# A new step order for an attention and gated feed-forward kernel, with the last value loads split in two

## The chip, the cores and the metric

The kernel runs on one core of a Trainium2 chip. The metric is the device time of one execution in microseconds (us). Time before: a median of 424.13 us over three runs (424.1, 424.13 and 425.38).

## The reference

Eight sequences of 448 tokens, twelve heads of 64. Queries and keys are normalised by their root mean square, attention follows, and its output (3584 rows of 768) goes through a feed-forward layer with a gate h * clip(h + 3, 0, 6) / 6 between two matrix products.

```python
q_n, k_n = rmsnorm(q, g_q), rmsnorm(k, g_k)               # q, k, v: (8, 12, 448, 64)
scores = matmul(q_n, k_n.transpose(0, 1, 3, 2)) / sqrt(64)
attn = softmax(scores)
x = matmul(attn, v) -> rows (8*448, 12*64)
h = x @ w_in                                              # (3584, 768) @ (768, 2048)
out = (h * clip(h + 3, 0, 6) / 6) @ w_out                 # (3584, 2048) @ (2048, 768)
```

## The kernel before

The unit of attention is a pair of heads; there are 48 pairs P, six for each sequence b. The kernel first builds a list of 2386 numbered steps (`Plan.add`), each with its kind, the engines that it may run on, and the steps that it depends on. Then `Plan.emit` puts them out in the order that the table `ORDER` gives; the table `WAY` says for a step which of its allowed engines it takes (0, the first one, if it isn't named). Every engine works off its own steps strictly in that order, so a step that waits holds up all that stands behind it on its engine. `ORDER` was written by a search outside the kernel; step numbers in this document are the numbers in these tables.

The kinds of steps that matter here:

- `ld`: SyncE (SP) issues one load of two heads' q, k or v, 256 KB (line 420). The order of loads on SP's queue is part of `ORDER`. q and k land in rings of six buffers `qk`, v in six buffers `vf`; for pairs 5 and 6 they land in space that later belongs to `gT` and `xT`.
- `sq`, `sqh` (squares, lines 362 on ACT and 364 on POOL), `red1`, `red2`, `redh` (sums, DVE, lines 449 and 483), `ln` and `ex` (the root by logarithm and exponential, ACT, lines 425 and 428), `sc`, `sch` (scaling, line 367, POOL or DVE): the normalisation of a pair.
- `tr`, `trh` (TensorE transposes, line 537) with `ck`, `cq` (copies out), and from pair 13 on `dt` (a DMA transpose issued by SP, line 556) with `kt` (a scaling of the keys in place on DVE or ACT, lines 566 and 564): the transposed q and k.
- `s` and `e`: scores of a block of keys on TensorE (lines 612 and 589) and their exponential on ACT (lines 617 and 595). The scores are two matmuls of 64 rows each, side by side in the array; every other matmul uses all rows.
- `cv`: the values to bf16 in `va` (line 346 on DVE, 348 on ACT, 352 on POOL), and `av`, `avh`: exponentials times values on TensorE (lines 675 and 634), then `rd`, `xn` (the division, DVE), and a transpose into `xT` (`xt`, `xth` on TensorE, `dx` by DMA, line 701).
- `h1`, `h3` (lines 748 and 767) with `relu` (ACT, line 726) and `gate` (DVE, line 729), `y384` (line 789) with `cy384` (copies on ACT or DVE, lines 348 and 350) and the store `st` (line 810): the feed-forward layer. Its matmuls fill TensorE's time between the attention steps of the next sequence.

The first sequence is done in two half passes over the queries (`prep_first`, `score_first`, `av_first`), so that TensorE gets work early; the weights are loaded by POOL meanwhile. Thirty `warm` matmuls on zeros run while nothing else is ready. Score banks (two, and a third one `X` shared with `av`) and two banks `M` for `h` and `y` are handed on by data dependencies: a score waits until `e` has read its bank, an `h3` until `gate` has.

Of the kernel before, what the change touches and what calls it, by code (L numbers as in the profile page):

```python
# [204 lines left out]
def kernel(  # L205
# [11 lines left out]
    nc = tc.nc  # L217
# [4 lines left out]
    NP = B * NPAIR  # L222
# [107 lines left out]
    for t in T_r:  # L330
        nc.vector.memset(t[:, S2:], 0.0)
    for t in eT_r:
        nc.vector.memset(t[:, :, S2:], 0.0)

    NPT = 13
    NXB = 2
    YA = 3
    NSP = 2
    NW0 = 8
    NW1 = 22  # L340

    plan = Plan()
# [65 lines left out]
    def load(P, parts=(0, 1, 2)):  # L408
        b, j = divmod(P, NPAIR)
        hs = slice(2 * j, 2 * j + 2)  # L410
        for i in parts:
            src = (q, k, v)[i]
# [544 lines left out]
```

## Time and profile before

| what | value |
|---|---|
| median of three runs | 424.13 us |
| the profiled execution | 425.55 us, of which the profile's span is 423.8 us |
| TensorE (PE) busy | 414.8 us, 98%, 3960 matmuls |
| ACT, DVE, POOL busy | 287.1, 225.8 and 178.1 us |
| granted TensorE clock over the span | 1.00 |
| data moved | 67.77 MB, 160 GB/s on average |
| fetches of instructions on queue q8 | 31 packets, 0.51 MB |

How to read it: an engine's share is an average over stages. TensorE is busy almost everywhere except at the very start, in a few stretches of the first 90 us and after the last matmul; ACT is busiest from 10 to 40 us and again around 100 us. The profile's marks such as `[1.55 <-DMA qk<-in_q_dram]` behind an instruction give the engine's idle time before it and what ended that. Busy times of matmuls overlap (they are pipelined), so a matmul's cost is taken below from the distance between the starts of neighbouring ones.

### The profile page before, as it was taken

Reading aid. Unit: us, or ns where it says so; the run is one execution under the profiler, and the core shown is the slowest. Engines: PE = TensorE matmul, PEld = TensorE weight load, DVE = VectorE, ACT = ScalarE, POOL = GpSimd, SP = SyncE. Lnnn points to the kernel's source line nnn. Section 1 sums busy time; section 2 is a strip of 40 time slices with the busy share of each in tenths; the row PEclk is TensorE's granted clock in tenths of the full one; section 3 lists DMA queues with packets and bytes.
Section 4 is the critical chain, followed back from the end, with each engine's and each line's share of the span. In section 5 each row is a group of like instructions: output and inputs, shape, how many; then the busy total and the mean of one; then the engine's idle time right before and its main releaser. Section 6 shows DMA issues by size and latency. Waiting matters only on the chain.

```text
span 423.8 us, 9991 instructions
## 1 busy us (share of the span) xinstructions
PE 414.8 (98%) x3960; PEld 243.0 (57%) x3960; DVE 225.8 (53%) x453; ACT 287.1 (68%) x523; POOL 178.1 (42%) x206
## 2 busy tenths in 40 slices
PE   7999999989999999999999999999999999999996
PEld 3566877645555555555555555555555555555564
DVE  5988774769775476565445455543453433232310
ACT  6999988789987768787767867666846662133101
POOL 3999685678774462593035655333030200000000
PEclk9999999999999999999999999999999999999999
DMA  7999999999869958595768469273144202200323
GB/s 249 292 282 220 244 216 170 274 267 274 207 155 267 249 129 226 172 197 144 198 154 239 110 159 215 79 184 77 40 106 112 57 26 60 43 7 0 109 68 118
DMA packets 98931, 67.77 MB, mean 160 GB/s; under 512 B 53156, under 2 KB 95428, under 8 KB 98884
## 3 DMA queue, kind: packets, MB, share of 16 engines
q1 hardware_dynamic: 93248, 60.50, 54.6%
q0 software_dynamic: 5248, 6.29, 9.0%
q8 instruction: 31, 0.51, 0.5%
q10 hardware_dynamic: 388, 0.34, 0.3%
q14 instruction: 16, 0.13, 0.1%
HBM read 50.23 MB, written 11.01 MB: 145 GB/s over the span
## 4 chain that ended last, share of the span: by engine, by line
PE 84%; DMA 6%; ACT 4%; issue 1%; DVE 1%; SPq 1%; POOL 1%; DVEq 0%; POOLq 0%; ACTq 0%
PE M L767 28%; PE M L789 27%; PE X L675 9%; PE S L589 5%; PE S L789 5%; PE X L589 3%; PE M L748 3%; DMA qk<-in_q_dram 3%; ACT eT L617 3%; DMA w_in_sb<-in_moe_w_in_dram 2%; DMA vf<-in_v_dram 1%; PE X L767 1%; PE S L767 1%; POOL qks L367 1%; PE X L789 1%
## 5 line engine op out<-in xcount | busy, mean ns | idle before, releaser
L367 POOL TENSOR_TENSOR qks<-qk,rs 112x512 bf16<-112x512 f32 (+1 forms) x88 | 88.9, 1024 | 119.5 <-ACT rs L428 94.8
L789 PE MATMUL M<-w_out_sb,gT 128*128 128x384 bf16 x752 | 138.0, 326 | 0.0
L767 PE MATMUL M<-xT,w_in_sb 128*128 128x448 bf16 x618 | 134.0, 353 | 0.0
L789 PEld LDWEIGHTS <-gT 128*128 128x128 bf16 x912 | 84.2, 98 | 58.3 <-issue 7.3
L729 DVE SCALAR_TENSOR_TENSOR gT<-ts,M 128x448 bf16<-128x448 f32 x119 | 73.3, 616 | 74.5 <-ACT ts L726 74.3
L595 ACT ACTIVATE eT<-S 112x896 bf16<-112x896 f32 x112 | 99.7, 916 | 6.9 <-PE X L675 3.6
L726 ACT ACTIVATE ts<-M 128x448 f32<-128x448 f32 x119 | 64.9, 546 | 46.5 <-PE M L767 39.4
L767 PEld LDWEIGHTS <-w_in_sb 128*128 128x128 bf16 x672 | 60.3, 98 | 58.2 <-issue 11.9
L364 POOL TENSOR_TENSOR sq<-qk 112x512 f32<-112x512 f32 (+1 forms) x59 | 59.1, 1012 | 24.1 <-DMA qk<-in_q_dram 9.6
L595 ACT ACTIVATE eT<-X 112x896 bf16<-112x896 f32 x56 | 51.3, 917 | 20.2 <-PE X L589 19.2
L675 PEld LDWEIGHTS <-eT 112*128 112x128 bf16 x1344 | 52.3, 97 | 15.1 <-DVE va L346 1.5
L675 PE MATMUL X<-va,eT 112*128 112x65 bf16 x1344 | 55.3, 193 | 1.4 <-DVE va L346 1.1
L449 DVE TENSOR_REDUCE ssq<-sq 112x16 f32<-112x1024 f32 x42 | 50.7, 1212 | 7.1 <-ACT sq L362 3.8
L589 PE MATMUL S<-T 64*128 64x448 bf16 x224 | 34.1, 353 | 0.1
L350 DVE COPY y<-M 128x384 f32<-128x384 f32 x23 | 12.8, 557 | 39.1 <-PE M L789 39.1
L694 DVE TENSOR_TENSOR xn<-X,rd 112x512 bf16<-112x512 f32 x42 | 28.9, 689 | 2.1 <-DMA xT<-xn 1.3
L691 DVE RECIPROCAL rd<-X 112x8 f32<-112x8 f32 x42 | 8.7, 207 | 38.2 <-PE X L675 35.4
L589 PEld LDWEIGHTS <-T 64*128 64x128 bf16 x336 | 12.3, 94 | 24.0 <-issue 18.8
L362 ACT ACTIVATE sq<-qk 112x512 f32<-112x512 f32 (+1 forms) x38 | 22.2, 595 | 5.6 <-DMA qk<-in_q_dram 3.4
L348 ACT COPY y<-M 128x384 f32<-128x384 f32 x24 | 11.5, 480 | 19.0 <-PE M L789 18.7
L748 PE MATMUL M<-xT,w_in_sb 128*128 128x224 bf16 x192 | 23.1, 259 | 0.2 <-DMA w_in_sb<-in_moe_w_in_dram 0.2
L789 PE MATMUL S<-w_out_sb,gT 128*128 128x384 bf16 (+1 forms) x128 | 22.3, 316 | 0.0
(88 smaller groups left out, 303.1 us busy)
## 6 DMA issues: line engine op xcount, KB each, us to landing
qk<-in_k_dram SPq DMA_DIRECT2D x45, 256.0 KB, 4.2
qk<-in_q_dram SPq DMA_DIRECT2D x45, 256.0 KB, 4.0
vf<-in_v_dram SPq DMA_DIRECT2D x45, 256.0 KB, 4.3
w_in_sb<-in_moe_w_in_dram POOLq DMA_DIRECT2D x4, 768.0 KB, 8.5
w_out_sb<-in_moe_w_out_dram POOLq DMA_DIRECT2D x4, 768.0 KB, 9.2
out_dram<-y SPq DMA_DIRECT2D x7, 336.0 KB, 3.9
out_dram<-y SPq DMA_DIRECT2D x8, 288.0 KB, 3.5
out_dram<-y SPq DMA_DIRECT2D x8, 240.0 KB, 2.7
```

The source lines that it names most:

```text
L364: em(nc.gpsimd.tensor_tensor(out=out, in0=in_, in1=in_, op=A_MULT))
L367: em((nc.vector if e == DVE else nc.gpsimd).tensor_tensor(out=out, in0=in_, in1=by.unsqueeze(3).to_broadcast(list(in_.shape)), op=A_MULT))
L449: em(nc.vector.tensor_reduce(out=ssq[:].rearrange("p i n -> p (i n)"), in_=sq[:].rearrange("p i (n d) -> p (i n) d", d=D), axis=AX_X, op=A ...
L589: em(nc.tensor.matmul(out=ps[:, a, 0:S], lhsT=qkT[r, S + t * TP:S + t * TP + 128], rhs=qkT[r, 0:S], start=True, stop=True))
L595: em(nc.scalar.activation(out=eT[:, t, 0:S2].rearrange("p (a s) -> p a s", a=2), in_=ps[0:TP, :, 0:S], func=EXP, bias=0.0, scale=1.0))
L675: em(nc.tensor.matmul(out=X_ps[:, a, i * E1:(i + 1) * E1], lhsT=eT[:, t, c:c + 128], rhs=va[:, a, t, :], start=(t == 0 and i == 0), stop=( ...
L694: em(nc.vector.tensor_tensor(out=xn[:].rearrange("p i a d -> p a i d"), in0=view()[:, :, :, 0:D], in1=rd[:].unsqueeze(3).to_broadcast([TP, ...
L726: em(nc.scalar.activation(out=ts[:], in_=ps()[:, 0:S], func=RELU, bias=0.5, scale=1.0 / 6.0))
L729: em(nc.vector.scalar_tensor_tensor(out=out, in0=shape(ts[:]), scalar=1.0, in1=shape(ps()[:, 0:S]), op0=A_MIN, op1=A_MULT))
L748: em(nc.tensor.matmul(out=ps()[:, f * SH:(f + 1) * SH], lhsT=w_in_sb[:, kt, f0:f0 + 128], rhs=xT[:, kt, z * SH:(z + 1) * SH], start=(kt == ...
L767: em(nc.tensor.matmul(out=ps()[:, 0:S], lhsT=w_in_sb[:, kt, f * 128:(f + 1) * 128], rhs=xT[:, kt, :], start=(kt == 0), stop=(kt == NKT - 1)))
L789: em(nc.tensor.matmul(out=ps()[:, 0:nc0], lhsT=gT[:, f, i * 128:(i + 1) * 128], rhs=w_out_sb[:, f, c0:c0 + nc0], start=(f == 0), stop=(f = ...
```

## The change

The list of steps and their dependencies stays as it was. Three things change.

1. `ORDER` and `WAY` are replaced by tables from another search, in a model that counts TensorE's instruction fetches and takes a third load that is issued right behind two others as late. Nearly all of the order differs in detail; the stages follow each other as before.
2. 123 steps run on another engine. The net of it: POOL gives away six `cv`, three `sq`, one `sqh` and two `sch` and takes two `sc`; ACT takes six `cv`, three `sq` and one `sqh` more; `kt` and `cy384` change engines in equal numbers.
3. The loads of v for the last three pairs (steps 1875, 1901 and 1927, pairs 45 to 47) become two DMAs each, one for each head.

```diff
     NPT = 13
     NXB = 2
+    NSL = 3
     YA = 3
...
-            def fn(_, dst=dst, src=src, np=np):
+            split = i == 2 and P >= NP - NSL
+
+            def fn(_, dst=dst, src=src, np=np, split=split):
                 rows = src[b, hs].rearrange("h (p t) d -> p h (t d)", t=T)
                 rows = bass.AP(rows.tensor, rows.offset, [[rows.ap[0][0], np]] + [list(d) for d in rows.ap[1:]])
-                em(nc.sync.dma_start(out=dst, in_=rows))
+                for h in ((0, 1) if split else (slice(0, 2),)):
+                    em(nc.sync.dma_start(out=dst[:, h], in_=rows[:, h]))
```

Some of what the tables change, by step. "Work ahead" is the TensorE work, in us, of all matmul steps that stand before the step in `ORDER`: the sum of their streaming times and 0.096 us for each change between scores and other matmuls.

| step | what it is | engine before, after | work ahead before | work ahead after |
|---|---|---|---|---|
| 10, 11 | loads of q and k of pair 1 | SP | 10 third, 11 fourth load | 11 third, 10 fourth load |
| 59, 60 | `ln`, `ex` for the first half of pair 0's queries | ACT | behind `sqh` 69 (reads load 10) | ahead of `sq` 68 (reads load 11) |
| 62 | `sch` of the same queries | POOL, DVE | 3.1 | 2.8 |
| 147 | load of v of pair 6 | SP | 20.5 | 20.1 |
| 346 | `cv` of pair 6 | DVE | 31.3 | 23.5 |
| 369 | load of v of pair 12 | SP | 71.6 | 65.3 |
| 589 | `cv` of pair 12 | DVE, POOL | 75.8 | 74.1 |
| 762 | first `av` of pair 12 | PE | 77.2 | 75.4 |
| 812 | `dt` of pair 16 | SP | 76.1 | 78.7 |
| 813 | `kt` of pair 16 | DVE | 81.9 | 82.8 |

Changes between scores and other matmuls in TensorE's order: 180 before, 170 after, 8 of the 10 fewer within the first 40 us of work.

279 rows, old and new, of tables (ORDER, WAY) are left out of this document.

## The prediction

> **What bounds the kernel now.** First the page: the span, TensorE's busy share, the slices.
>
> ```profile
> span 423.8 us, 9991 instructions
> ...
> PE 414.8 (98%) x3960; PEld 243.0 (57%) x3960; DVE 225.8 (53%) x453; ACT 287.1 (68%) x523; POOL 178.1 (42%) x206
> ...
> PE   7999999989999999999999999999999999999996
> ```
>
> TensorE is the bound, and a new order takes no matmul away. So I measured what an order can touch: from the starts of all 3960 matmuls I took each form's shortest distance to the next start (189 ns for an `h3` matmul, 161 for `y384`, 29 for `av`). Their sum is 384.8 us. The first matmul starts at 1.2, the last at 419.8; the 33.6 us between sum and reality are all there is. Part of that is the change between the scores' 64-row matmuls and the others, in the timeline of TensorE:
>
> ```profile
> 117.59 0.35 PE L589 MATMUL S<-T 64*128 64x448 bf16 x2
> 117.88 1.31 PE L767 MATMUL M<-xT,w_in_sb 128*128 128x448 bf16 x6
> 119.12 0.36 PE L589 MATMUL X<-T 64*128 64x448 bf16 x2
> ```
>
> Two scores side by side take 0.29 us to the next start instead of 0.19, six L767 1.24 instead of 6 x 0.189 = 1.13: some 96 ns a change. 180 changes x 0.096 = 17.3 us. The remaining 16.3 us lie, by start: 5.1 before 16 us, 1.9 to 28, 1.8 to 40, 1.2 to 60, 0.4 to 80, 1.6 to 100, and 4.2 thinly over the rest (no single wait above 0.12). The chain of waits, in order of time, names the two places with a cause:
>
> ```profile
> 1.77 5.09 DMA qk<-in_q_dram
> ...
> 82.44 6.31 DMA vf<-in_v_dram
> 89.61 1.15 PE X L675 x32
> ```
>
> The first, in the timeline of the start:
>
> ```profile
> 6.88 0.42 ACT L362 ACTIVATE sq<-qk 112x256 f32<-112x256 f32 x1 [1.55 <-DMA qk<-in_q_dram]
> 7.20 0.19 ACT L425 ACTIVATE rs<-ssq 112x4 f32<-112x4 f32 x1
> ...
> 8.38 0.47 PE L537 MATMUL M<-identity,qks 112*128 112x112 bf16 x6 [1.05 <-POOL qks L367]
> ```
>
> Load 10, the third, lands 5.1 us after issue; the first two took 2.7 and 2.9. `sqh` 69 waits for it 1.55 us at the head of ACT's queue, and `ln` 59, whose sum was there at 5.49, stands behind. The second is the largest single wait after 16 us:
>
> ```profile
> 88.86 0.69 DVE L346 TENSOR_SCALAR_CACHE_REDUCE va<-vf 112x512 bf16<-112x512 f32 x1 [2.35 <-DMA vf<-in_v_dram]
> ...
> 89.61 0.57 PE L675 MATMUL X<-va,eT 112*128 112x65 bf16 x13 [1.08 <-DVE va L346]
> ```
>
> Load 369 was issued at 82.44, too late for `cv` 589; TensorE lost 1.26 us by the starts. The stretches show what bounds the early stage:
>
> ```profile
> 10.00:20.00 10.00, 9.18 (x124) 5.11 (x126) 9.68 (x25) 9.94 (x26) 8.55 (x12) 1.00 1.07 307
> 20.00:30.00 10.00, 9.85 (x184) 6.71 (x182) 8.28 (x29) 9.90 (x17) 9.23 (x14) 1.00 0.98 263
> 30.00:40.00 10.00, 9.32 (x146) 6.71 (x142) 8.26 (x25) 9.71 (x17) 9.94 (x11) 1.00 1.10 246
> ```
>
> The columns after the length are PE, PEld, DVE, ACT, POOL, clock, DMA share, GB/s: ACT is full from 10 to 40 us, TensorE's "busy" there includes waits.
>
> **The change, part by part.** The sum is made against the profiled execution (425.55, of which 423.8 span); the median is 1.42 lower, and I carry the difference over to it.
>
> *Early stage, to about 44 us.* In the new order `ln` 59 and `ex` 60 stand ahead of the first reader of the third load, and `sch` 62 moves to an idle DVE. The first transposes come perhaps 1.3 us earlier. But ACT still restarts only with the third load, and it is the full engine. So I added up ACT's queue from that point, each step by its spacing back to back (`e` 0.80, `sq` 0.52, `sqh` 0.31, `ck` 0.52, `cv` 0.51, `relu` 0.42, `ln` and `ex` 0.11). Up to `e` step 536, at 43.71 before: 34.58 us of queue in 36.83 elapsed, so 2.25 of slack. New queue to the same step: 35.17. Bounds: all slack gone, 6.88 + 35.17 = 42.05, a gain of 1.66; all slack kept, a loss of 0.59. Slack was 0.9 by 23 us, where ACT is fullest; the rest came after. I take a third of it closed: -0.75 + 0.59, say **-0.2**. The 8 mode changes fewer here hide behind ACT.
>
> *The value load of pair 6.* `cv` 346 on DVE moves from 31.3 to 23.5 us of TensorE work, load 147 hardly. Between the load's issue and `cv` ACT has five `e` and three roots, 4.3 us, where 11.8 us lay between the two before. Loads around 28 us landed in 5.3 to 6.0 us. So DVE should wait 1.0 to 1.7 us at step 346, and behind it are `cq` 375, `rd` 335, `xn` 336, `ck` 377, which feed TensorE's next steps. DVE is 83% busy there and part is made up. Bounds 0 and 1.7; I take **+0.5**, as the loads that compete may also be fewer by then.
>
> *44 to 87 us.* 1.6 us less the switches' share remain, the largest 0.46 at 54.13 (an `av` waiting for `e`). The new order has POOL some 2.5 us of steps ahead at 60 us. Bounds 0 and -1.4; half of it, **-0.7**.
>
> *The wait at 88 us.* From load 369 to `cv` 589 there were 4.2 us of TensorE work (6.4 by the clock) against a landing of 6.31; now 8.8. The wait goes: **-1.2**. Next late: `dt` 812 to `kt` 813, 5.8 us of work before and 4.1 now, while that transpose landed in 5.1. DVE may wait up to 1.0 us, with the `gate` steps behind it that free the `M` banks. Bounds 0 and 1.0, **+0.3**.
>
> *After 90 us.* Mode changes there and in the two stretches before: two fewer, **-0.2**. The shortest distances in TensorE's order are alike in both: `gate` to the next `h3` on its bank 1.50 and 1.50 us, `e` to `av` 1.04 and 1.04, a copied `y` bank to the next `h3` 0.76 and 0.76; none of them stalled before. ACT takes over six `cv` (0.51) and three `sq` (0.52), 4.6 us of 287; from 100 to 120 us it is 95% busy, but `e` runs 8.6 us of work or more ahead of the `av` that frees it for reuse. Bounds 0 and +0.5, taken as 0.
>
> *The split loads.* Three more issues of about 0.47 us on SP's queue, with stores and `dx` behind them; the readers stand 12.3, 6.1 and 27.7 us of work behind, and the whole loads landed in 2.9 to 3.9. Nothing waited for them and nothing will: **0**. If the cover were gone, an issue costs 0.47. The tail (last matmul to the end, 3.9 us) has the same last fifteen steps, in an order that differs in a few copies and stores: 0.
>
> *Instruction fetches.* Queue q8 moves 31 packets of 16 KB, at 42.93, 49.63, 61.09 and so on. I find no TensorE gap at them: outside the mode changes no distance after 100 us is over 15 ns too long. So an order that avoids them gains 0. [...]
>
> Sum: -0.2 + 0.5 - 0.7 - 1.2 + 0.3 - 0.2 = -1.5. 425.55 - 1.5 = 424.05 for a profiled execution, 424.13 - 1.5 = **422.6 us** for the median.
>
> **Rivals.** A measurement of this kernel tells about 0.3% from no change, 1.27 us here: faster means below 422.86, slower above 425.4.
>
> *Given back (no change).* The wait at 88 us goes, but the DVE waits at 346 and 813 take their upper halves (1.2 and 0.7), and the 44 to 87 stretch gains only a third: -0.2 + 1.2 - 0.5 - 1.2 + 0.7 - 0.2 = -0.2, so 423.9. For it: both landings are measured longer than the new leads. Against: the old order was itself tight (`dt` 663 to `kt` 664 had 3.06 us for a landing of 3.0) and did not wait.
>
> *Blocked load issue (slower).* SP's seventh load in a row took long to issue:
>
> ```profile
> 25.16 1.70 SPq L420 DMA_DIRECT2D qk<-in_k_dram  x1
> ...
> 28.45 0.47 SPq L420 DMA_DIRECT2D xT<-in_v_dram  x1
> ```
>
> The new order issues seven loads in a row before 147 in the same stretch. If one of them blocks by 1.7 us, 346 waits 2.7 to 3.4 us, DVE makes up perhaps 0.8, and the early gain is gone with it: +0.6 (ACT's longer queue) + 2.3 - 0.5 - 1.2 + 0.3 - 0.2 = +1.3, 425.4, and with the upper wait 425.8. It decides from a TensorE loss of about 2.3 us at 346. Against: with its reader only 3.5 us of work behind, the new model holds a third load to be late and still puts `cv` there.
>
> *Nothing reached.* The waits are set by data, not order, and only the one at 88 us goes: about 422.9 to 423.3, counted with no change.
>
> **Numbers.** Forecast and neighbours below 422.86: 0.53. No change, from the first and third rival: 0.30. Slower: 0.17. Range 420.8 to 425.5: downwards the early slack wholly closed (-1.66 for -0.2) and half of the rest; upwards the blocked load.
>
> **What would show it.** Right: `ln` 59 before any `sq` that reads loads 10 or 11; the first L537 near 7 us; no wait of `av` 762; the last three v loads twice as many DMAs with no waiter; TensorE's distances after 100 us unchanged. Wrong: DVE idle over 1.5 us at L346 around 32 us with TensorE waiting for `rd`, `xn` or `ck`; `e` step 536 later than 44.3; DVE idle at L566 near 92 us. The prediction as a whole is wrong if the start of `av` 762, 89.61 before, moves by less than 0.8 us, or if gaps appear at places that no row here shows.

## The result, and the profile after

The changed kernel takes 426.64 us (median of 22 executions, 425.02 to 430.86) against 425.37 for the kernel before, measured alongside: a ratio of 1.0044, 95% interval 1.0026 to 1.0061. (The ratios here and below are those on record; the quotient of these two medians is 1.0030, that of the means 1.0045.) It is slower. The forecast was 422.6, so the median lies outside the range and on the other side. Of the 4.0 us between them 1.2 are the base: the forecast started from a median of three runs, 424.13, and 22 runs of before give 425.37. The change itself was forecast as -1.5 us and came as +1.3 (by the medians) to +1.9 us (by the ratio).

The profiled execution of after is the longest of its 22: 430.86 us, of which 429.1 are the span. Sizes read from it are upper ends, so a second profile of the same kernel (427.96 us, span 426.2, below as "after again") stands beside it wherever a size matters. The page of after, with the slices of TensorE (PE) and of its granted clock:

```profile
span 429.1 us, 9978 instructions
...
PE   8997999999999999999998999999999999999997
...
PEclk9998999999999999999999999999999999999999
```

Apart from the first and the last slice, the one under nine tenths was the ninth (85 to 95 us) before; now they are the fourth (32 to 43 us), where the granted clock is short too, and the 22nd (225 to 236 us). The timeline of that stretch, with the load of v of pair 6 (step 147) on SP's queue, its reader `cv` 346 on DVE (L348 now), the score 397 on TensorE and its exponential:

```profile
27.33 0.47 SPq L425 DMA_DIRECT2D xT<-in_v_dram  x1
...
33.88 0.69 DVE L348 TENSOR_SCALAR_CACHE_REDUCE va<-xT 112x512 bf16<-112x512 f32 x1 [2.25 <-DMA xT<-in_v_dram]
...
34.93 0.37 PE L617 MATMUL S<-gT 64*128 64x224 bf16 x4 [2.31 <-DVE T L352]
...
35.33 0.92 ACT L622 ACTIVATE eT<-S 112x896 bf16<-112x896 f32 x1 [2.19 <-PE S L617]
```

The load lands 6.5 us after its issue. DVE has been standing at step 346 for 2.25 us by then, the copy `cq` 375 that score 397 needs is queued right behind it, and so TensorE loses 2.31 us and ACT, the full engine of this stage, 2.19. Before, nothing waited for this load. Then comes something that no row of before showed. Windows over the stretch (columns as before: length, PE, PEld, DVE, ACT, POOL, clock, DMA share, GB/s):

```profile
32.00:34.00 2.00, 0.62 (x21) 0.59 (x18) 0.12 (x1) 1.14 (x3) 1.39 (x3) 1.00 1.13 343
34.00:36.00 2.00, 0.89 (x14) 0.64 (x14) 1.68 (x6) 0.67 (x1) 1.39 (x3) 1.00 1.18 198
36.00:38.00 2.00, 1.79 (x26) 1.05 (x25) 1.75 (x6) 1.81 (x4) 1.83 (x2) 0.79 1.23 204
38.00:40.00 2.00, 2.00 (x28) 1.60 (x26) 1.10 (x4) 1.56 (x4) 0.05 (x1) 0.50 1.24 206
40.00:42.00 2.00, 2.00 (x20) 1.00 (x18) 1.62 (x6) 1.26 (x2) 2.00 (x3) 0.86 1.24 206
```

Two microseconds after the wait has ended, TensorE's clock falls to half (0.50) and stays there until 40.6 us.

At the other place that the prediction named, the wait has become smaller: the first `av` of pair 12 (step 762) waits 0.41 us in place of 1.08 by the timeline, behind `cv` 589, which is on POOL now and follows another late value load there:

```profile
90.21 1.17 POOL L354 CAST va<-vf 112x512 bf16<-112x512 f32 x2 [1.89 <-DMA vf<-in_v_dram]
...
91.44 0.65 PE L680 MATMUL X<-va,eT 112*128 112x65 bf16 x16 [0.41 <-POOL va L354]
```

To see where time goes in any of the kernels I compare TensorE at equal work. For each matmul step I take the sum of the streaming times of all steps ahead of it in that kernel's order (386.2 us in all, mode changes not counted), and subtract it from the step's start: the lag. The table gives each kernel's lag minus that of before's profile, in us; "front" and "rest" are the hybrids of the experiments below.

| work done, us | after | after again | load 147 early | front of before, rest of after | before, load 369 early |
|---|---|---|---|---|---|
| 8 | -1.02 | -0.78 | -0.78 | -0.54 | -0.36 |
| 20 | -0.28 | -0.02 | +0.13 | -0.56 | -0.37 |
| 24 | +3.45 | +2.54 | +0.32 | -0.82 | -0.66 |
| 42 | +2.97 | +2.32 | -0.24 | -1.30 | -1.07 |
| 65 | +3.55 | +2.85 | +0.23 | -1.12 | -1.08 |
| 70 | +2.86 | +1.58 | -1.03 | -2.27 | -2.30 |
| 100 | +4.41 | +2.96 | +0.54 | -1.05 | -2.30 |
| 200 | +4.67 | +3.07 | +0.93 | -0.73 | -2.30 |
| 300 | +5.80 | +2.89 | +1.55 | -0.91 | -2.30 |

The last two columns run before's own order up to 42 us of work and still differ from before's profile by 0.4 to 1.3 there: so much single executions scatter in the first stages. Both are also profiles of short executions (424.15 and 423.23 us, medians 425.31 and 424.63), so their last rows are not what these kernels gain. Three things stand out: the jump from 20 to 24 us in the two columns of after, the 1.2 us won from 65 to 70 in nearly every column, and the 1.2 to 1.6 given back from 70 to 100 wherever the rest is that of after.

### The profile page after: what moved, and what is told of

It reads as the page before. It is cut to its first block, busy times and chain, and to the rows that moved or that the text cites. A ratio compares the mean times of both kernels' runs of the same rounds, so it can differ in the third digit from the quotient of the medians.

```text
span 429.1 us, 9978 instructions
## 1 busy us (share of the span) xinstructions
PE 416.7 (97%) x3960; PEld 244.2 (57%) x3960; DVE 225.6 (53%) x454; ACT 291.7 (68%) x532; POOL 171.5 (40%) x196
## 4 chain that ended last, share of the span: by engine, by line
PE 74%; DMA 11%; ACT 6%; POOL 3%; issue 2%; SPq 1%; DVE 1%; POOLq 0%; ACTq 0%; DVEq 0%
PE M L772 26%; PE M L794 23%; PE X L680 8%; PE S L594 5%; PE S L794 4%; DMA w_out_sb<-in_moe_w_out_dram 3%; ACT eT L622 2%; PE X L594 2%; DMA out_dram<-y 2%; DMA xT<-in_v_dram 2%; POOL qks L369 1%; DMA qk<-in_k_dram 1%; DMA vf<-in_v_dram 1%; DMA T<-qks 1%; PE X L772 1%
## 5 line engine op out<-in xcount | busy, mean ns | idle before, releaser
L794 PE MATMUL M<-w_out_sb,gT 128*128 128x384 bf16 x752 | 140.0, 326 | 0.5 <-DMA w_out_sb<-in_moe_w_out_dram 0.5
L369 POOL TENSOR_TENSOR qks<-qk,rs 112x512 bf16<-112x512 f32 (+1 forms) x89 | 90.1, 1028 | 110.2 <-ACT rs L433 78.7
L366 POOL TENSOR_TENSOR sq<-qk 112x512 f32<-112x512 f32 (+1 forms) x55 | 55.4, 1017 | 50.7 <-DVE gT L734 22.4
L594 PE MATMUL S<-T 64*128 64x448 bf16 x224 | 35.1, 357 | 1.4 <-ACT eT L600 1.4
L364 ACT ACTIVATE sq<-qk 112x512 f32<-112x512 f32 (+1 forms) x42 | 24.4, 593 | 3.0 <-DMA qk<-in_k_dram 2.9
```

Source lines behind the costliest of these rows:

```text
L364: em(nc.scalar.square(out=out, in_=in_))
L366: em(nc.gpsimd.tensor_tensor(out=out, in0=in_, in1=in_, op=A_MULT))
L369: em((nc.vector if e == DVE else nc.gpsimd).tensor_tensor(out=out, in0=in_, in1=by.unsqueeze(3).to_broadcast(list(in_.shape)), op=A_MULT))
L594: em(nc.tensor.matmul(out=ps[:, a, 0:S], lhsT=qkT[r, S + t * TP:S + t * TP + 128], rhs=qkT[r, 0:S], start=True, stop=True))
L794: em(nc.tensor.matmul(out=ps()[:, 0:nc0], lhsT=gT[:, f, i * 128:(i + 1) * 128], rhs=w_out_sb[:, f, c0:c0 + nc0], start=(f == 0), stop=(f = ...
```

## The experiments

Theory: `cv` 346 was moved ahead of where its load can have landed; with DVE standing at it, TensorE starves and its clock falls. Rivals: the value loads split in two, or the new order as a whole, make the loss. Each table below lists ratios against runs of before measured alongside. In all kernels `_move(i, j)` takes step i out of `ORDER` and puts it right ahead of step j.

### The value load of pair 6 from both ends

The first takes the load to an earlier place in after:

```diff
+_move(147, 228)
```

> The new order with one load moved: load 147 (v of pair 6) stands ahead of load 228 on SP's queue, third of its row instead of eighth. Theory 1 (a load that lands late under a reader at the head of DVE's queue): the load is issued near 24 us and lands by 30, cv 346 no longer waits (under 0.3 us at its line against 2.25), TensorE's wait ahead of score step 397 falls from 2.3 to under 0.6 us, the granted clock stays at 1.00 from 36 to 42 us where it fell to 0.50, and the time falls by 2 us or more against the new order, to a ratio of 0.995 to 1.001 against the kernel before. Theory 2 (ACT's longer queue sets the early stage): the wait moves to ACT, e step 536 stays later than 45.5 us, and the ratio stays at 1.004.

The second leaves the load and takes the reader back:

```diff
+_move(346, 513)
```

> The new order with one reader moved: cv 346 stands ahead of step 513 on DVE (near 42 us), the load stays where the new order has it. Theory 1: cq 375, rd 335 and ck 377 no longer stand behind a wait, TensorE's wait ahead of step 397 falls under 0.6 us, the clock stays at 1.00, ratio 0.995 to 1.001; the first av of pair 6 (step 516) starts no later than its exponential allows. Theory 2: as in the run with the load moved, 1.004. If this run and the one with the load moved give the same, it is the pair of load and reader and not the load on the DMA queues.

The third keeps order and engines of after and takes the split loads away:

```diff
-    NSL = 3
+    NSL = 0
```

> The new order with the last three v loads in one DMA each. All theories: the same as the new order within 0.2% (ratio to the kernel before about 1.004), since nothing waited for these loads. It also gives a second profile of the new order: theory 1 expects DVE to wait 1 to 2.5 us for load 147 again, and the granted clock to fall after it only where TensorE waited some 2 us or more; a rival (the clock falls by itself in some runs) expects low clock at another place or none with the same wait.

The fourth is before, with that one reader moved forward:

```diff
+_move(346, 375)
```

> The kernel before with one step moved as the new order has it: cv 346 stands ahead of cq 375 on DVE instead of 6 us later; its load 147 is issued at 28.45 as before. Theory 1: DVE waits for the load from about 32.5 until 34.4, TensorE loses 1.5 to 2.5 us ahead of step 397, perhaps with a lower clock behind it (another 1 us), ratio 1.004 to 1.009. Theory 2 (that place is harmless, ACT sets the pace): DVE makes the wait up, at most +0.5 us, ratio under 1.002.

| kernel | median, us | ratio, 95% interval | executions with a clock under 0.998 |
|---|---|---|---|
| after, load 147 early | 425.78 | 1.0006, 0.9985 to 1.0026 | 1 of 12 |
| after, `cv` 346 late | 426.09 | 1.0002, 0.9983 to 1.0021 | 0 of 12 |
| after, no split loads | 426.86 | 1.0030, 1.0007 to 1.0052 | 3 of 12 |
| before, `cv` 346 early | 427.98 | 1.0041, 1.0015 to 1.0066 | 8 of 12 |

Either end undoes the loss, and one moved step puts as much into the kernel before. The waits of that last kernel from 28 to 36 us (us in total, times, longest), and its windows:

```profile
PE S L619 <- DVE T L357: 2.0, 1, 2.0
...
DVE va L353 <- DMA xT<-in_v_dram: 1.4, 1, 1.4
```

```profile
34.00:36.00 2.00, 1.83 (x22) 1.13 (x22) 1.79 (x8) 1.44 (x2) 1.98 (x3) 0.86 1.20 190
36.00:38.00 2.00, 2.00 (x18) 1.46 (x18) 1.42 (x2) 1.44 (x2) 1.39 (x2) 0.50 1.19 192
38.00:40.00 2.00, 2.00 (x35) 1.50 (x34) 1.07 (x6) 1.39 (x5) 0.45 (x1) 0.79 1.19 193
```

It is the picture of after: wait, then half the clock. With load 147 early the largest wait of a matmul for DVE in this window is 0.4 us, and the clock is 1.00 from 28 to 42:

```profile
PE S L624 <- DVE T L367: 0.4, 1, 0.4
```

The split loads are not what makes the loss: without them the time stays above before, with an interval that overlaps that of after.

That kernel also gives a third profile of the same order around the load. I had expected a DVE wait of 1 to 2.5 us in it; it was 0.64, the score 397 waited 0.73, and the clock did not fall:

```profile
32.69 0.69 DVE L348 TENSOR_SCALAR_CACHE_REDUCE va<-xT 112x512 bf16<-112x512 f32 x1 [0.64 <-DMA xT<-in_v_dram]
...
33.74 0.37 PE L617 MATMUL S<-gT 64*128 64x224 bf16 x4 [0.73 <-DVE T L352]
```

The three side by side, with the lag at 24 us of work against the same order with the load early:

| profile | load 147 lands in, us | DVE waits, us | TensorE waits at 397, us | clock falls | lag, us |
|---|---|---|---|---|---|
| after | 6.5 | 2.25 | 2.31 | yes | 3.1 |
| after again | 5.2 | 0.91 | 0.99 | yes | 2.2 |
| after, no split loads | 5.2 | 0.64 | 0.73 | no | 0.7 |

But both repaired kernels only equal before; the gains that the prediction counted on are not there, and the last group of runs asks why.

### The clock

If TensorE's idle time sets off the fall, matmuls on zeros in the wait should prevent it. Their results are read by nobody.

```diff
+        n = len(plan.ops)
...
                         skip_group_check=True))
+            if n == 353:
+                idle(56, X0_r[x])
```

First in before with `cv` 346 early, then in after, beside after again:

> The order of before with the value copy 346 moved ahead of step 375 on DVE (that kernel took 427.98 us, and in 8 of 12 executions the granted clock was 0.996 or less), and 56 more matmuls on zeros behind step 353, 33 ns apart in the trace, 1.85 us in all, so that TensorE works while 346 waits for its load. They change no result that is read. If the clock falls because TensorE has stood idle for about 2 us: TensorE's wait at step 397 shrinks to under 0.3 us, no execution or one has a clock under 0.998, the windows at 35 to 40 us show 1.00, and the time falls by the share of the slow clock, 8 of 12 times some 1.2 us: about 427.1 us, still 1.4 above before, as the load's lateness stays. If the clock falls for another reason (a burst on the engines after the wait, or how the chip is at the time): the clocks stay as they were, most under 0.997, and the time is 428 us or more.

> After with 56 more matmuls on zeros behind step 353 (1.85 us by their distance of 33 ns), whose results nobody reads; order and engines are those of after. The value load stays as late as it is, only TensorE does not stand idle. If the fall of the clock is set off by TensorE's idle time and costs about 1 us where it happens: no execution under a clock of 0.998, and 0.4 to 0.8 us less than after in the same comparison (after: 9 of 22 executions with a lower clock). If the clock costs nothing on the median: the same time as after within 0.3 us. If the fall has another cause: lower clocks as often as in after.

> After itself, unchanged, beside the kernel with the busy TensorE. By the first comparison: 1.0044 of before (1.0026 to 1.0061), some 4 in 10 executions with a clock under 0.998, and those about 2 us longer than the others. If the profiled execution of after, the longest of its 22, was out of the ordinary, the wait at step 397 in this profile is nearer to 1 us than to 2.3.

| kernel | median, us | ratio, 95% interval | clock under 0.998 |
|---|---|---|---|
| before, `cv` 346 early, busy | 427.78 | 1.0063, 1.0042 to 1.0085 | 1 of 6 |
| after, busy | 427.39 | 1.0053, 1.0034 to 1.0072 | 0 of 6 |
| after again | 427.83 | 1.0047, 1.0020 to 1.0074 | 8 of 12 |

Windows of after again, and of the busy kernel:

```profile
32.00:34.00 2.00, 1.01 (x30) 0.95 (x26) 1.16 (x5) 1.38 (x3) 1.39 (x3) 1.00 1.14 357
34.00:36.00 2.00, 1.61 (x29) 1.20 (x26) 1.46 (x6) 1.73 (x3) 2.00 (x4) 0.92 1.11 181
36.00:38.00 2.00, 2.00 (x23) 1.26 (x21) 1.44 (x2) 1.28 (x3) 1.43 (x2) 0.50 1.22 203
```

```profile
32.85 1.80 PE L375 MATMUL XF<-zero_t 128*128 128x64 bf16 x56
...
34.58 0.36 PE L617 MATMUL S<-gT 64*128 64x224 bf16 x4
```

```profile
32.00:34.00 2.00, 2.00 (x66) 1.96 (x64) 1.25 (x5) 1.52 (x4) 1.39 (x2) 1.00 1.06 311
34.00:36.00 2.00, 1.61 (x41) 1.27 (x36) 0.91 (x5) 1.02 (x2) 2.00 (x4) 1.00 1.08 175
36.00:38.00 2.00, 2.00 (x43) 1.46 (x40) 1.75 (x4) 1.94 (x4) 1.57 (x2) 1.00 1.20 193
```

The load is late in both (DVE waits 0.91 and 0.86 us for it); the idle time is filled in one, and there the clock stays whole. Over all runs: 1 of 12 executions of the two busy kernels has a lower clock, against 25 of 46 of the same orders without the filler (17 of 34 of after, 8 of 12 of before with 346 early) and 3 of the 110 executions of before whose clock is on record. So the idle time sets off the fall. What it costs I can only bracket. By the lag, after again goes from -0.02 at 20 us to +2.54 at 24, and 1.06 us of that is the wait at score 397 (by the starts; 0.99 by the timeline): up to 1.5 for the clock and small waits under it. Before with 346 early goes from -0.76 to +2.21 with 2.04 of wait: 0.9.

The single times say more than the medians. The 34 executions of after fall into two groups that do not overlap: 17 with a clock of 0.998 or more take 425.02 to 426.98 us (median 426.23), 17 with a lower one 427.51 to 430.86 (median 428.53). So an execution of after without the fall is some 0.9 us above before's 425.37, one with it 3.2. The 2.3 us between the groups are the clock together with whatever longer wait went with it, so they are more likely an upper end for the clock alone than its price.

On the median, the busy kernel is only 0.44 us under after again, and by the ratios not under it at all; the intervals overlap, and the forecast of 427.1 for the first busy kernel was missed by 0.7. In the profile shown, the filler itself runs on 0.75 us after `cq` 375 has ended (33.8), so it takes back part of what the clock gives. How much of the 2.3 us is the clock is not settled.

### Where the forecast gains went

The two orders hold nearly the same set of steps after step 569 of before (step 553 of after), at about 48 us, so they can be joined there. The hybrids have the code of after; engines come from the kernel whose part a step is in.

```diff
-ORDER = (after)
+ORDER = (before up to step 569) + (the remaining steps in the order of after)
```

> Steps in the order and on the engines of before up to its step 569 (about 48 us), then in the order and on the engines of after. If the whole loss of after lies at its value load of pair 6: no wait there, so before's time less the wait at 88 us (1.26) and less most of the mode changes (0.9): 423.6 to 424.6 us. If the new order is also the tighter one behind 50 us (its small waits at y384 461, av 788, s 834, av 846, s 1030, h3 957 and the late transpose 1672, 0.3 to 0.8 us each, add 1.5 to 2.9 us to what it saves): slower than before by 1 to 2 us, 426.5 to 428 us, with a granted clock of 1.00 throughout.

```diff
-ORDER = (after)
+ORDER = (after with load 147 early, up to step 553) + (the remaining steps in the order of before)
```

> Steps in the order and on the engines of after, with load 147 ahead of load 228, up to step 553 (about 48 us), then in the order and on the engines of before. If the early start of after is worth what its first score is earlier in the profiles (1.0 us): 424.7 us or less. If the stretch to 33 us goes at ACT's pace in both orders, so that an earlier start only becomes ACT's queue: within 0.4 us of before (425.3 to 425.8 us), with the wait at av 762 in the profile as in before (1.0 to 1.5 us).

The wait at 88 us by itself, in before:

```diff
+_move(369, 499)
```

> Before with one edit: load 369 issued ahead of load 499, at about 80.4 us in place of 82.4, with 499, 534, 746 and 655 one place later each. If the wait of 1.26 us at av 762 is worth its length: no wait at av 762, and 1.0 to 1.3 us less than before (some 424.5 us). If it is given back at once by what is late next: cv 589 no longer waits for its load, but PE waits 0.3 us or more at another step between 89 and 100 us, and the time is 425.2 to 425.8 us, the same as before. If the four loads that move back by 0.5 us each are then late (653 on DVE reads load 499): a new wait of DVE or POOL for a load, and the time is that of before or more.

> The same kernel as before with load 369 moved ahead of load 499, run again, since its first ratio of 0.9985 had an interval from 0.9969 to 1.0001. If its gain is the wait of 1.26 us at av 762: a ratio between 0.997 and 0.999 again, no wait at av 762. If the first run was chance: a ratio of 0.9995 to 1.0005.

| kernel | median, us | ratio, 95% interval |
|---|---|---|
| front of before, rest of after | 425.31 | 1.0004, 0.9986 to 1.0021 |
| front of after, rest of before | 424.54 | 0.9985, 0.9971 to 1.0000 |
| before, load 369 early | 424.63 | 0.9985, 0.9969 to 1.0001 |
| the same again | 425.03 | 0.9984, 0.9969 to 0.9999 |

The first hybrid came between its two expectations (423.6 to 424.6, or 426.5 to 428). Before with one load moved is, with the second hybrid, the fastest kernel of the case: two measurements agree on 0.15 to 0.16% less, some 0.65 us, the second with an interval just below 1. That is about half of the 1.0 to 1.3 us expected. A likely reason, not shown, is that the wait at 88 us is not the same in every execution of before's order: `av` 762 waited 1.08 us in before's profile, 1.18 in that with `cv` 346 early and 0.36 in the busy one. The timeline of before with one load moved has the two value copies of that stretch on DVE, neither with a wait:

```profile
85.35 0.67 DVE L353 TENSOR_SCALAR_CACHE_REDUCE va<-vf 112x512 bf16<-112x512 f32 x1
...
86.06 0.69 DVE L353 TENSOR_SCALAR_CACHE_REDUCE va<-vf 112x512 bf16<-112x512 f32 x1
```

Its lag falls by 1.22 us from 65 to 70 us of work and nothing is given back. The front of after with the rest of before gains about as much, and by the same step of the lag (from +0.05 at 65 us to -1.17 at 70): I had expected its 88 us wait to remain, wrongly, since TensorE reaches `av` 762 later there after 0.72 us of wait for a weight (`w_out` 7) at 74 us. The early start of after adds nothing visible here, so that the number expected of this hybrid (424.7 or less) came true without the early start for which it was expected.

The rest of after wins the same 1.15 us and is even with before in the end. The timeline of ACT in that hybrid shows one way in which it goes:

```profile
88.73 0.67 ACT L557 ACTIVATE T<-T,gp_t 128x448 bf16<-128x448 bf16 x1 [1.41 <-DMA T<-qks]
89.31 0.61 ACT L352 ACTIVATE sq<-qk 112x512 f32<-112x512 f32 x1
89.83 0.61 ACT L338 CAST va<-vf 112x512 bf16<-112x512 f32 x1
90.34 0.63 ACT L352 ACTIVATE sq<-qk 112x512 f32<-112x512 f32 x1
90.87 0.89 ACT L588 ACTIVATE eT<-X 112x896 bf16<-112x896 f32 x1
```

ACT stands 1.41 us at `kt` 761 for a transpose, then has a square, a `cv` and a square to do before the exponential 785; `kt` 761, `cv` 776 and `sq` 853 came over from DVE and POOL. TensorE loses 0.46 us at `av` 788 and 0.35 at score 834. I tried to take that back, first alone in this hybrid, then in after together with its other named waits, then the latter once more in the right order:

```diff
+_move(626, 563)
+_move(760, 626)
+WAY[776] = 2
+WAY[853] = 0
```

> The kernel with the front of before and the rest of after (425.31 us), in which ACT stood 1.41 us at 88.7 us for the transpose 760 (issued 81.54, landed 7.1 us later) and then had kt 761, a square, cv 776 and sq 853 in front of the exponential 785, so that av 788 and score 834 waited 0.46 and 0.35 us and score 806 0.2. Here transpose 760 is issued before loads 626, 563 and 746 instead of after them, cv 776 is on DVE and sq 853 on GpSimd, as both were in before. If this late transpose and the steps that came over from DVE and GpSimd to ACT are what eats the gain of the 88 us stretch: ACT's wait is under 0.4 us, the three waits of PE are gone, and the time is 0.7 to 1.0 us less, 424.3 to 424.6 us. If the gain is lost to something else and the next wait only steps in: 425.0 to 425.6 us, the same as before.

```diff
+_move(147, 228)
+_move(7, 647)
+_move(1673, 1917)
+_move(626, 563)
+_move(760, 626)
+WAY[776] = 2
+WAY[853] = 0
```

> After with all the repairs: load 147 ahead of load 228 (that one alone took 425.78 us); w_out 7 issued ahead of the square 647 on GpSimd (y384 461 waited 0.4 us for it); transpose 760, cv 776 and sq 853 as in the run above (0.7 us of waits of av 788 and score 834); kt 1673 half a round later on ACT, ahead of square 1917 (in the profile of after it stood 2.0 us at ACT's head for its transpose and PE lost 1.3). If the losses of after are separate waits of steps that stand at an engine's head before their load, weight or transpose has landed, each can be taken away by its own move: 424.0 to 424.8 us, some 0.3% under before. If the order is tight all over, so that one wait removed lets the next one step in: 425.4 to 426 us, like before.

```diff
+_move(6, 647)
 _move(7, 647)
```

> As the kernel with all the repairs, but with both w_out 6 and w_out 7, in this order, issued ahead of the square 647 on GpSimd. There w_out 7 went ahead of w_out 6, so that y384 455, which needs w_out 6 first, waited 3.35 us. If the losses of after are separate waits, each of a step that stands at an engine's head before its load, weight or transpose has landed: no wait at y384 455 or 461, none at score 1666 near 234 us, and 424.4 to 425.0 us, 0.2% under before. If the order is tight all over, so that the next wait steps in: 425.4 to 426.2 us, like before and like the kernel with load 147 moved alone.

| kernel | median, us | ratio, 95% interval | clock under 0.998 |
|---|---|---|---|
| hybrid, ACT relieved | 426.06 | 0.9999, 0.9977 to 1.0020 | 2 of 12 |
| after, repaired, `w_out` 7 ahead of 6 | 429.62 | 1.0100, 1.0069 to 1.0130 | 6 of 6 |
| after, repaired, in order | 425.85 | 1.0021, 1.0002 to 1.0041 | 1 of 12 |

The hybrid with ACT relieved loses nothing at 788 and 834 any more (its lag falls by 0.49 us from 65 to 95 us of work, where the hybrid before stayed level), although `av` 846 in that stretch now waits 0.61 us for `cv` 744 on POOL. It gives the gain back from 100 to 130 (+0.95 against +0.40), with 0.3 us at score 1086 and 0.5 at `h3` 957 by the starts. The repaired kernel in order has no wait at 1666 over 0.5 us and none at 788 or 834. It still waits 0.45 at `y384` 461 for `w_out` 7, and 1.3 us by the starts (1.17 by the timeline) at `av` 846, whose `cv` 744 stands on POOL behind a square that waits for DVE:

```profile
104.38 1.04 POOL L380 TENSOR_TENSOR sq<-qk 112x512 f32<-112x512 f32 x1 [1.53 <-DVE gT L748]
105.36 0.61 POOL L368 CAST va<-vf 112x512 bf16<-112x512 f32 x1
```

So I was wrong with the sum of separate waits: the repairs at 397, 788 and 834 took their waits away, those at 461 and 1666 only a part, and the next tight step stepped in. 424.4 to 425.0 was expected, 425.85 came. The middle kernel's edit put `w_out` 7 ahead of `w_out` 6, which `y384` 455 needs first. That mistake made a clean case for the clock, with the longest wait of all, and the clock low in every execution:

```profile
72.00:74.00 2.00, 0.04 (x2) 0.07 (x1) 0.00 (x0) 2.00 (x3) 1.01 (x2) 1.00 0.97 172
74.00:76.00 2.00, 0.68 (x4) 0.43 (x4) 0.00 (x0) 0.23 (x1) 0.00 (x0) 0.95 0.88 278
76.00:78.00 2.00, 2.00 (x34) 1.89 (x33) 0.00 (x0) 0.00 (x0) 0.00 (x0) 0.50 1.06 251
78.00:80.00 2.00, 2.00 (x12) 0.61 (x10) 1.81 (x3) 0.12 (x1) 0.00 (x0) 0.70 0.99 268
```

## Why the prediction was wrong, step by step

**The step that failed and turned the sign is the value load of pair 6**, taken as +0.5 us with bounds of 0 and 1.7. By the ratios, 1.0044 against 1.0006 with the load early, it cost some 1.6 us (1.2 by the medians, each against its own before). By the lag at 24 us of work it was 0.7 us where the clock stayed whole and 2.2 and 3.1 where it fell. The mechanism was there, with the right steps behind it (`cq` 375 first). Two things were mis-sized. I let DVE make up part of the wait, but the step right behind it was what TensorE needed next, so nothing was made up: DVE's waits of 0.64, 0.91 and 2.25 us became 0.73, 0.99 and 2.31 at score 397. And the upper bound did not contain the clock, 0.9 to 1.5 us in the two traces that allow an estimate. The landings, put at 5.3 to 6.0 us, were not the fault: 5.1 to 5.5 in four profiles with the load at this place, 6.5 in the longest execution alone.

**The other gains failed by more.** Without the value load the sum was -2.0 us; the kernels with that load repaired measured 1.0006 and 1.0002, about +0.1 to +0.3 us. That is some 2.2 us too much hope, against 1.1 for the value load. The terms follow below.

The rival **Blocked load issue**, with a chance of 0.17, came near in its total by luck. An issue in the run ahead of load 147 did block, and not in the longest execution alone: of the two loads in each of these rows one takes 1.35 us (after, the first row) and 1.39 us (after again), and 1.2 to 1.3 in the three other profiles with load 147 at this place (no split loads, `cv` 346 late, busy).

```profile
23.31 1.92 SPq L425 DMA_DIRECT2D qk<-in_k_dram  x2
...
23.55 1.96 SPq L425 DMA_DIRECT2D qk<-in_k_dram  x2
```

Load 147 went out at 27.3 to 27.7 us in all five. Of the four whose reader stands early, DVE waited 0.64 to 0.91 us in three, where the rival counted 2.7 to 3.4. The point that it gave for deciding, 2.3 us of TensorE loss, was met in the longest execution by 2.31; but there the load was issued earliest of all (27.33) and landed late (6.5 us). Its argument against itself, that the search's model knows a third load to be late, was no evidence. It counted a change of +1.3 to +1.7 us, against +1.3 to +1.9 measured, made up of other parts. Its upper end, 425.8, also lay above the 425.5 that the prediction gave as the end of its range.

**Early stage, -0.2.** Nothing was won. `ln` 59 does come first, and the first L542 is near 7 us, as forecast:

```profile
5.47 0.30 ACT L430 ACTIVATE rs<-ssq 112x4 f32<-112x4 f32 x2 [1.21 <-DVE ssq L488]
...
6.99 0.47 PE L542 MATMUL M<-identity,qks 112*128 112x112 bf16 x6
```

But half of the 1.7 us between the two profiles at `ln` 59 belonged to the one execution of before that I read. In before with `cv` 346 early, whose start is that of before, ACT waited 0.44 us for load 10 in place of 1.55, and in five more profiles with that start 0.37 to 0.61:

```profile
5.96 0.42 ACT L369 ACTIVATE sq<-qk 112x256 f32<-112x256 f32 x1 [0.44 <-DMA qk<-in_q_dram]
6.29 0.19 ACT L432 ACTIVATE rs<-ssq 112x4 f32<-112x4 f32 x1
```

Seven profiles with before's start have their first exponential at 9.08 to 9.87 us, nine with after's at 9.12 to 9.81. And at 42 us of work five kernels with after's front and a repaired value load stand between -0.65 and +0.63 (-0.24 with the load early, -0.41 with `cv` late, -0.64 repaired), on average -0.26, those with before's front on average -0.44 (five, scattered from -1.30 to +0.53). This fits the view that ACT's queue decides here; eight of the ten mode changes saved lie in this stage, and no gain from them is visible, as forecast.

**44 to 87 us, -0.7.** Measured from 42 to 65 us of work: +0.58, +0.53 and +0.47 in the first three columns, +0.18 in the hybrid with the rest of after, -0.01 in before with load 369 early. What came in the three is `y384` 461 waiting for `w_out` 7, about 0.5 us by the starts; `h3` 429 waiting for `gate` 420 (0.5 to 0.9 us) stands just ahead of that stretch. Taking half of the possible gain, without looking at how tight the new order's own steps are, was the fault.

**The wait at 88 us, -1.2.** Right for the profile: -1.15 to -1.27 from 65 to 70 us in all kernels that were not disturbed there, and -0.69 in after, where 0.58 of it stayed. Over the executions it is worth less, as before with load 369 early shows (0.65 us).

**The next late, +0.3.** The place was right, the size is a matter of the execution. `kt` 813 followed the step ahead of it on DVE without a gap in after, after again and with the load early; with `cv` 346 late it waited 2.48 us for its transpose, more than twice the upper bound. The division `xn` stands right behind it on DVE, and the score that waits for `xn` lost 1.94 us:

```profile
97.28 0.68 DVE L578 TENSOR_SCALAR_CACHE_REDUCE T<-T,gp_t 128x448 bf16<-128x448 bf16 x1 [2.48 <-DMA T<-qks]
...
98.62 0.37 PE L601 MATMUL X<-T 64*128 64x448 bf16 x2 [1.94 <-DVE xn L706]
```

Without the split loads and in the busy after it waited 0.69 and 0.65. What was not in the sum at all is `av` 788 and score 834 behind ACT (0.3 to 0.5 and 0.36 us by the starts) and `av` 846 behind `cv` 744 (0.4 to 0.6): the columns with the rest of after lose 1.2 to 1.6 from 70 to 100 us.

**After 90 us, -0.2.** Even in the hybrid (+0.14 from 100 to 300). In after, one more late transpose, `dt` 1672 issued at 226.82 and read by `kt` 1673 too early; the waits from 225 to 240 us:

```profile
ACT T L569 <- DMA T<-qks: 2.0, 1, 2.0
PE S L594 <- ACT eT L600: 1.2, 1, 1.2
```

This was not in the sum. After again did not have it (its lag stays level from 200 to 300), the busy after did (1.1 us by the starts). "TensorE's distances after 100 us unchanged" was therefore wrong for some executions.

**Split loads and instruction fetches, 0.** Both right: four DMAs of 128 KB and two of 112 KB, nobody waits for them; queue q8 still moves 31 packets.

Of the signs named for a wrong prediction, these came: `av` 762 did not start earlier (91.44 and 90.16 us in the two profiles of after, 89.61 before); `e` 536 started later than 44.3 (46.54 and 45.50); gaps appeared at places that no row of before showed; and, in the longest execution alone, DVE was idle over 1.5 us at the value copy near 32 us with TensorE waiting. One sum of the prediction is off by a little: 419.8 - 1.2 - 384.8 is 33.8 us, not 33.6, and nothing hangs on it.

## What to carry to other kernels

Where engines work off their queues in order, a step that reads a load is priced by what stands right behind it, not by its own wait: look up the two next steps on its engine, and if the bound engine needs one of them at once, count the whole lateness of the load, plus the chance of a lower clock (here in half of the executions, with 1.0 and 2.3 us of wait in the two profiles). One profiled execution is not the typical one: of the 1.55 us that I set out to remove at the start, six other profiles had 0.37 to 0.61, and the three profiles of the new order put the cost of the same late load at 0.7, 2.2 and 3.1 us. And in an order this tight a removed wait is not worth its length in the profile: one load moved by four places took away 1.2 us there and gained 0.65 us over the executions, and a whole new order that removed the same wait gained nothing.

## What the runs showed of the hardware

In the four profiles with a low stretch inside the kernel, the granted clock fell to 0.50 after TensorE had waited 0.99, 1.96, 2.31 and 3.28 us by the timeline. The kernels of the first three had a lower clock in 25 of 46 executions, that of the longest wait in 6 of 6. The length of the wait alone does not decide: the clock did not fall in the profile of the kernel with `cv` 346 late, where TensorE stood idle for 1.9 us near 97 us, nor after the 1.2 us at score 1666 in after. In windows of half a microsecond, the low stretch lasted 3.41 us in after again, 3.42 in after, 3.41 in before with 346 early and 3.41 in the repaired kernel with the swapped weights. It began 0.5 to 2.2 us after the wait had ended. What else decides whether the clock falls in an execution was not shown: the same order had it in 17 of 34.
